# Pacing the second round of V loads with the heads in a cached-attention forward and backward kernel

## Chip, cores, metric

One core of a Trainium2 chip. The metric is device time in microseconds for one execution. All kernels here give the correct result.

## The reference

Gradients of one decode step of an adaLN block: attention with a KV cache, then a gated FFN. What fills the time is the cache:

```
x: (2, 1, 512)   k_cache, v_cache: (2 batches, 32 heads, 8192, 128) bf16, 128 MiB each
q = h @ wq;  p = softmax(q k^T / sqrt(128));  o = p v;  x = x + ga * (o @ wo);  x = x + gb * ffn(...)
returned: the output and the gradients of x, k_cache, v_cache, wq, wo, w1, w3, w2, c, w_mod
```

The gradient of each cache is as large as the cache: per head 2 MB of dV and 2 MB of dK are stored. V is needed twice, for o and again for the gradient of p, so all but two heads of V are loaded a second time.

## The kernel before

The program is laid out in slots, eight to a head. Heads of "job a" read K and V (forward). Heads of "job c" read V again and store dV and dK (backward). Between them stand two "chains", one per batch, that turn the attention output into the gradients that job c needs. After the second chain (slot t1 = 784) only job c is left: 32 heads in slots 768 to 1023, beside about 200 small tasks (weight gradients, which go out through staging tiles "stg").

All big data passes through 21 half tiles (1 MB each: half a head of K, V, dV or dK). Loads are issued by SP, in the order of need, as soon as the bookkeeping of the program has a free half tile (beyond a few that `keep` holds back for the stores):

```python
def load_v(key, i, hf):
    t = htile()
    qd.dma_start(t[:], src_of(A_v_cache, i)[:, hf * HK:(hf + 1) * HK, :])
    free["half"] -= 1
    V[(key, hf)] = t

def pump():
    while loads and free["half"] - keep[0] >= 1:
        loads.pop(0)[2]()          # (slot of need, sequence, load)
```

PE transposes V of the head (eight 128x128 blocks a slot), the half tile is then free. DVE makes dV and dK as outer products into other half tiles, and POOL stores them:

```python
def transposes(block, dve):
    tp = tps.tile([P, GRP, P], BF16, name="tp", tag="tp")
    for j in range(GRP):
        nc.tensor.transpose(tp[:, j, :], block(j), identb[:])
    kt = ktp.tile(...)                      # copied by ACT, or DVE in 2 slots of 8
def outer(store, dst, n, which, w2, q):
    ...                                     # cut
    nc.vector.tensor_tensor(...)            # 128x2048 outer product, two to a half tile
    if o + QK == HK:
        sq_.dma_start(src_of(dst, n)[...], t[:])       # sq_ is POOL
        at(now[0] + 6, PL_FREE, back)       # the half tile counts as free 6 slots later
def chain_done():                           # at slot t1
    ...                                     # the chain's weights give their half tiles back
    pump()
def again(w, n):                            # weights once more, for two last gradients
    for pc in range(n - 1, -1, -1):
        loads.insert(0, (0, 0, lambda pc=pc: load_piece(wqr, w, pc)))    # need 0: first in line
    pump()
```

By this bookkeeping the loads run 53 slots, over six heads, ahead of their use from slot 787 on: at t1 there is a burst of nine V loads, and afterwards about 13 of the 21 half tiles hold V that waits.

## Time and profile before

| | before |
|---|---|
| median of the first 6 runs | 1759.84 us (1757.52 to 1761.74) |
| profiled run | 1758.21 us, span 1756.4 us |
| bytes moved | 713.59 MB |

From the page of the kernel before: the busy share of the DMA engines in 40 slices of the span, what they moved, and the two big queues (q1 are the loads, q0 the stores).

```profile
DMA  9999999999999999999999999999999999999997
GB/s 381 418 417 416 418 417 390 418 377 414 382 411 422 413 414 410 420 410 409 410 413 409 409 420 403 382 371 419 424 413 419 409 405 417 413 421 423 420 402 293
q1 hardware_dynamic: 73376, 425.81, 60.0%
q0 software_dynamic: 41216, 284.22, 39.1%
```

The DMA is full from end to end: nothing else bounds this kernel.

From the kernel's waits, 1260 us to the end: who waited for whom, us in total, times, longest.

```profile
DVE half L1038 <- DMA out_dram<-half: 83.8, 40, 5.0
ACT stg L1163 <- DMA out_dram<-stg: 76.5, 20, 14.8
```

DVE waits 84 us for stores to land, because the loads hold most half tiles.

### The profile page before, as it was taken

What the parts mean: (1) busy time and instruction counts of PE and PEld (TensorE: products, weight loads), DVE (VectorE), ACT (ScalarE), POOL (GpSimd) and SP (SyncE); (2) the same over time, 40 slices, a digit from 0 to 9 for tenths busy, and PEclk for the clock granted to TensorE, in tenths of its full rate; (3) what the DMA queues carried; (4) which work ended last, traced back from release to release, by engine and by line L of the source; (5) the groups of instructions that cost most, each with busy time, mean ns of one, the idle gap of its engine ahead of it and who ended that gap; (6) DMA issues with size and microseconds to landing.
All of it is one profiled execution on the core that took longest, in us unless ns stands there. A gap on an engine that the chain in (4) does not pass through costs nothing. (4 is left out here: it accounts for less than half of the span.)

```text
span 1756.4 us, 55279 instructions
## 1 busy us (share of the span) xinstructions
PE 1371.6 (78%) x24266; PEld 1224.9 (70%) x24266; DVE 1181.3 (67%) x1697; ACT 953.2 (54%) x1370; POOL 391.6 (22%) x685
## 2 busy tenths in 40 slices
PE   5999999989887776668677767887678777866862
PEld 5999998888876666667576666787555555664662
DVE  2666665856767667667766767899566666665695
ACT  4666665653654454555455455434465566664762
POOL 0333333310222122222212222211012221111121
PEclk7999999989986888898888889668665555585785
DMA  9999999999999999999999999999999999999997
GB/s 381 418 417 416 418 417 390 418 377 414 382 411 422 413 414 410 420 410 409 410 413 409 409 420 403 382 371 419 424 413 419 409 405 417 413 421 423 420 402 293
DMA packets 114847, 713.59 MB, mean 406 GB/s; under 512 B 11392, under 2 KB 20300, under 8 KB 33196
## 3 DMA queue, kind: packets, MB, share of 16 engines
q1 hardware_dynamic: 73376, 425.81, 60.0%
q0 software_dynamic: 41216, 284.22, 39.1%
q8 instruction: 190, 3.11, 0.7%
q14 instruction: 53, 0.43, 0.1%
q10 hardware_dynamic: 12, 0.01, 0.0%
HBM read 425.79 MB, written 284.20 MB: 404 GB/s over the span
## 5 line engine op out<-in xcount | busy, mean ns | idle before, releaser
L371 ACT COPY kt<-tp 128x1024 bf16<-128x1024 bf16 x768 | 775.2, 1015 | 587.7 <-PE tp L366 574.3
L366 PE MATMUL tp<-identb,half 128*128 128x128 bf16 x8192 | 759.4, 248 | 4.2 <-DMA half<-in_A_k_cache_dram 1.9
L366 PEld LDWEIGHTS <-half 128*128 128x128 bf16 x8192 | 590.0, 111 | 113.6 <-issue 109.4
L1043 POOL DMA_DIRECT2D out_dram<-half x256 | 136.3, 532 | 983.0 <-DVE half L1038 798.9
L427 PE MATMUL m_ps<-ek,half 128*128 128x129 bf16 x4096 | 327.3, 222 | 0.2 <-DMA half<-in_A_v_cache_dram 0.2
L369 DVE COPY kt<-tp 128x1024 bf16<-128x1024 bf16 x256 | 176.2, 688 | 182.8 <-PE tp L366 181.1
L1015 PE MATMUL s_ps<-DO_bf,kt 128*128 128x1 bf16 x4096 | 190.1, 167 | 102.6 <-DVE kt L369 60.0
L1015 PEld LDWEIGHTS <-kt 128*128 128x128 bf16 x4096 | 184.4, 106 | 119.3 <-DVE kt L369 67.0
L386 PE MATMUL s_ps<-qT_bf,kt 128*128 128x1 bf16 x4096 | 177.8, 164 | 107.0 <-DVE kt L369 100.9
L427 PEld LDWEIGHTS <-half 128*128 128x128 bf16 x4096 | 247.8, 98 | 0.4 <-DMA half<-in_A_v_cache_dram 0.4
L386 PEld LDWEIGHTS <-kt 128*128 128x128 bf16 x4096 | 160.3, 98 | 113.0 <-DVE kt L369 105.0
L1163 ACT CAST stg<-m_ps 128x512 bf16<-128x512 f32 (+2 forms) x123 | 72.1, 592 | 107.7 <-DMA out_dram<-stg 76.5
L1162 PE MATMUL m_ps<-half 2*128 2x512 bf16 (+2 forms) x123 | 72.2, 587 | 23.5 <-ACT stg L1163 21.9
L449 PE MATMUL k_ps<-half,pz 128*32 128x512 bf16 x1024 | 67.4, 383 | 24.7 <-POOL pz L435 24.7
L449 PEld LDWEIGHTS <-pz 128*32 128x32 bf16 x1024 | 21.6, 96 | 45.3 <-POOL pz L435 27.0
L1263 ACT COPY kt<-tp 128x1024 bf16<-128x1024 bf16 x28 | 28.7, 1043 | 11.1 <-PE tp L1256 11.1
L398 DVE TENSOR_REDUCE nm<-s_ps 128x1 f32<-128x128 f32 x64 | 18.6, 290 | 20.1 <-PE s_ps L395 20.1
L1140 ACT CAST half<-m_ps 2x512 bf16<-2x512 f32 (+1 forms) x36 | 20.0, 564 | 22.4 <-DVE ds_26107 L1059 9.0
L1256 PE MATMUL tp<-identb,half 128*128 128x128 bf16 x224 | 21.6, 254 | 12.6 <-DMA half<-in_A_wq_dram 8.2
L395 PE MATMUL s_ps<-nident,rm 128*128 128x128 bf16 x64 | 14.8, 232 | 18.2 <-DVE rm L390 18.2
L1256 PEld LDWEIGHTS <-half 128*128 128x128 bf16 x224 | 16.7, 114 | 12.9 <-DMA half<-in_A_wq_dram 8.5
L714 DVE COPY kt<-tp 128x1024 bf16<-128x1024 bf16 x32 | 22.1, 690 | 4.2 <-PE tp L711 4.2
(870 smaller groups left out, 1792.3 us busy)
## 6 DMA issues: line engine op xcount, KB each, us to landing
out_dram<-half POOLq DMA_DIRECT2D x256, 1024.0 KB, 13.4
half<-in_A_v_cache_dram SPq DMA_DIRECT2D x252, 1024.0 KB, 12.5
half<-in_A_k_cache_dram SPq DMA_DIRECT2D x128, 1024.0 KB, 19.8
out_dram<-stg POOLq DMA_DIRECT2D x22, 512.0 KB, 16.8
half<-in_A_wq_dram SPq DMA_DIRECT2D x8, 1024.0 KB, 17.0
half<-in_w_mod_dram SPq DMA_DIRECT2D x6, 1024.0 KB, 16.6
half<-in_B_w_dram SPq DMA_DIRECT2D x6, 1024.0 KB, 15.4
half<-in_A_wo_dram SPq DMA_DIRECT2D x4, 1024.0 KB, 20.5
```

What stands on the lines that cost most here:

```text
L366: nc.tensor.transpose(tp[:, j, :], block(j), identb[:])
L369: nc.vector.tensor_copy(kt[:], tp[:])
L371: nc.scalar.copy(kt[:], tp[:])
L386: nc.tensor.matmul(S_ps[i][:, cc:cc + 1], kt[:, j, :], qT_bf[:, h, b:b + 1], start=True, stop=True)
L427: nc.tensor.matmul(m[:, 0:P + 1], vb_(i, kk), t[:, kk % QK, 0:P + 1], start=(kk == 0), stop=(kk == KK - 1), skip_group_check=True)
L449: nc.tensor.matmul(kp["ps"][NR * j:NR * (j + 1), :], pz[:, o:o + NR], K[(i, kk // HK)][:, kk % HK:kk % HK + QP, :], start=False, stop=(h = ...
L1015: nc.tensor.matmul(DP[n][:, cc:cc + 1], kt[:, j, :], DO_bf[:, b, h:h + 1], start=True, stop=True)
L1043: sq_.dma_start(src_of(dst, n)[:, hf * HK:(hf + 1) * HK, :], t[:])
L1162: nc.tensor.matmul(ps[:lw, 0:rw], rsl(ln, lc, lw), rsl(rn, rc, rw), start=True, stop=True)
L1163: nc.scalar.copy(st["t"][:lw, o:o + rw], ps[:lw, 0:rw])
L1256: nc.tensor.transpose(tp[:, k * NC + kc, :], piece(wqr, kc, m0 + k), identb[:])
L1263: nc.scalar.copy(kt[:], tp[:])
```

## The change

Its intent: after the second chain, load V only as it is needed, in lots of four half tiles, at most 12 slots (a head and a half) ahead, the first of each lot tied by a semaphore to the last PE transpose before it in the program. Half tiles are then left to the stores. The diff, whole but for the lines that only keep handles of the last load and the last transpose:

```diff
+    LOT = 4
+    AHEAD = NG + NG // 2              # NG is 8
+    paced = [False]
+
     def pump():
+        if paced[0] and loads and loads[0][0] > 0:
+            if loads[0][0] > now[0] + AHEAD:
+                return
+            if free["half"] - keep[0] < min(LOT, len(loads)) and loads[0][0] > now[0] + HG:
+                return
+            for k in range(min(LOT, len(loads), free["half"] - keep[0])):
+                issued[0] = None
+                loads.pop(0)[2]()
+                if k == 0 and issued[0] is not None:
+                    tc.add_manual_dep(issued[0].ins, turned_last[0].ins.name, ...,
+                                      reason="loads keep pace with the heads")
+            return
         while loads and free["half"] - keep[0] >= 1:
             loads.pop(0)[2]()
 ...
@@ def chain_done():
             rowst[k] = hflat()
             free["half"] -= 1
+        paced[0] = True
         pump()
```

In words: V loads due more than 12 slots ahead are held back, and so is a lot until four half tiles are free (unless its first load is due within HG, which is 4 slots).

At t1 V is in hand up to slot 804, so no load is due until slot 796: the burst of nine is gone. And a weight reload has need 0, so while one is first in line the old greedy path runs and takes V loads along: five V loads too early at slots 903 and at 954.

More of the change, by code (lines that the diff above doesn't have):

```diff
@@ L163 @@
     V = {}
+    issued = [None]
+    turned_last = [None]
     def src_of(ap, i):
@@ L176, in load_v @@
         t = htile()
-        qd.dma_start(t[:], src_of(A_v_cache, i)[:, hf * HK:(hf + 1) * HK, :])
+        issued[0] = qd.dma_start(t[:], src_of(A_v_cache, i)[:, hf * HK:(hf + 1) * HK, :])
         free["half"] -= 1
@@ L327, in want @@
         loads.append((need, seq[0], f))
+    LOT = 4
+    AHEAD = NG + NG // 2
+    paced = [False]
     def pump():
+        if paced[0] and loads and loads[0][0] > 0:
[7 more added lines that the diff above has]
+                if k == 0 and issued[0] is not None:
+                    tc.add_manual_dep(issued[0].ins, turned_last[0].ins.name,
+                                      mybir.DependencyInfo(mybir.DependencyClass.Sync, mybir.DependencyReason.DATA),
+                                      reason="loads keep pace with the heads")
+            return
         while loads and free["half"] - keep[0] >= 1:
@@ L365, in transposes @@
         for j in range(GRP):
-            nc.tensor.transpose(tp[:, j, :], block(j), identb[:])
+            turned_last[0] = nc.tensor.transpose(tp[:, j, :], block(j), identb[:])
         kt = ktp.tile([P, GRP, P], BF16, name="kt", tag="kt")
```

## The prediction

> **What bounds the kernel now.** The DMA. The utilisation slices show the DMA engines at 90% or more in 39 of 40 slices; the queue table gives 60.0% of the span to loads, 39.1% to stores. 713.59 MB must move whatever the order: at the best rate of any stretch (426 GB/s, 1260 to 1300 us, windows view) that is 1675 us; the span is 1756. PE is busy 78%, DVE 67%, ACT 54%.
>
> The change acts only after the second chain, in the last 490 us, where 32 heads each load 2 MB of V and store 4 MB. Windows view: 1260-1300: 426 GB/s, DMA 1.01; 1300-1650: 414 GB/s, 1.01, DVE busy 222 of 350; 1690-1750: 364 GB/s, 0.89, stores only, DVE busy 48 of 60. The last V load is issued at 1654.5 us, 100 us before the end: the slot bookkeeping lets loads run 53 slots (over six heads, 13 of the 21 half tiles) ahead. Stores have few half tiles left: in the waits view from 1260 us, DVE waits 84 us for earlier stores to land. This is not lost time: the DMA is full meanwhile.
>
> **What the change does.** No work or bytes change. It (a) holds V loads to 12 slots ahead, so some eight half tiles move from waiting V to stores in flight; (b) issues loads in lots of four, the first of each tied to a PE transpose; (c) leaves the greedy path while weight reloads wait, so the pacing breaks twice.
> - DVE's 84 us of waits should mostly go, into a longer store queue (landing 17 us now, perhaps 20 to 35). Worth about 0 with the DMA at 1.01.
> - A head costs about 16 us of DMA (6.3 MB plus weight gradients at 414 GB/s); DVE's own work is eight products of 1.22 us plus copies, about 12 us. So 12 slots ahead is 18 to 25 us (estimate), against 10.9 us median landing of a V load. PE should rarely wait for V.
> - Loads mixed into the end: stores alone ran at some 395 GB/s for 55 us (estimate from the last window without its empty end), mixed at 414 to 426: 2 to 4 us gained.
> - The burst of nine loads just after the chain goes; stores alone must fill the DMA for 12 slots, DVE-limited near 350 GB/s (4.2 MB per 12 us): 2 to 3 us lost.
> - Weight-gradient staging waits behind a deeper store queue (ACT already waits 76 us for it): 0 to 3 us lost.
>
> The Trainium skill, "DMA: Bandwidth & Descriptors", section "Queues, rings and completion order", says each engine takes turns between queues by packet; the trace roughly agrees (1260-1300: 7.47 MB loaded, 9.50 MB stored). So a lot of four is not stuck behind a deep store queue.
>
> **Prediction.** 1756 us, range 1744 to 1769. Faster by over 2%: 1%; within 2%: 95%; slower by over 2%: 4%.
>
> **What would show it.** Right: DMA share about 1.0 from 1300 us on, V loads issued until some 40 us before the end, DVE's wait for store landings well under 84 us, store landing over 17 us, end windows over 364 GB/s, PE waiting on V under 10 us. Wrong: windows with DMA share below 0.95, or PE transposes released by V loads.
>
> **What would make it wrong.** Slower: V loads land later than 12 slots because their buffers' stores have not landed, or the staging stores stall ACT and with it the transposes, so that the DMA runs dry between lots. Faster: lots of four and deeper store queues raise the mixed stretch from 414 towards 426 GB/s (up to 12 us), which I do not expect, since 50/50 and 25/75 mixes look nearly alike.

## More of the kernel before

From the kernel before, the last 560 us; in each row the stretch and its length, busy time (and instructions) of PE, PEld, DVE, ACT and POOL, then the granted PE clock, the DMA share and GB/s.

```profile
core 0: us, PE busy (x) PEld busy (x) DVE busy (x) ACT busy (x) POOL busy (x), PEclk, DMA share, GB/s
1200.00:1240.00 40.00, 32.22 (x544) 30.64 (x544) 36.34 (x78) 17.69 (x25) 5.31 (x10) 0.71 1.01 424
1240.00:1270.00 30.00, 17.94 (x264) 15.24 (x262) 14.86 (x18) 12.96 (x21) 3.19 (x6) 0.67 1.01 425
1270.00:1450.00 180.00, 137.42 (x1477) 101.20 (x1477) 114.00 (x121) 107.62 (x179) 35.55 (x62) 0.54 1.01 411
1450.00:1650.00 200.00, 147.52 (x1821) 114.38 (x1819) 124.81 (x139) 124.04 (x187) 33.42 (x63) 0.61 1.02 418
1650.00:1690.00 40.00, 30.65 (x600) 28.71 (x599) 30.75 (x34) 30.64 (x41) 6.37 (x12) 0.84 1.00 414
1690.00:1770.00 80.00, 26.65 (x480) 25.10 (x478) 48.02 (x50) 23.08 (x31) 10.10 (x19) 0.70 0.67 273
```

(The span ends at 1756.4, so the last row is 66 us of work and an empty rest.) The rate hardly leaves 411 to 425 GB/s before the stores-only end.

## The result, and the profile after

| | before | after |
|---|---|---|
| median | 1759.18 us (20 runs, 1756.47 to 1763.58) | 1766.54 us (10 runs, 1758.79 to 1768.92) |
| ratio | | 1.0034, 95% interval 1.0022 to 1.0046 |
| profiled run | 1758.21 us | 1760.47 us |

Ratios, here and below, are the mean time of one kernel's fast runs over the mean of the other's from the same rounds, so not quite the ratio of the medians.

The kernel is a third of a per cent slower: inside the predicted range, on the other side of zero than its centre. Its runs lie in two clusters, three at 1758.8 to 1761.5 us and seven at 1765 to 1769 us; the profiled run is of the shorter one.

The page of the kernel after, the same two lines of slices:

```profile
DMA  9999999999999999999999999999999999999997
GB/s 382 417 417 417 418 417 389 418 377 408 382 408 423 419 422 417 406 413 411 416 414 414 407 409 410 384 370 418 365 419 412 417 412 420 423 423 422 369 424 322
```

The digits are the same, the rates are not: slice 29 fell from 424 to 365 GB/s and slice 38 from 420 to 369. The windows of the kernel after (same columns):

```profile
1200.00:1240.00 40.00, 32.52 (x548) 30.97 (x546) 35.45 (x77) 16.29 (x21) 5.53 (x11) 0.69 0.98 409
1240.00:1270.00 30.00, 26.80 (x426) 22.59 (x425) 29.49 (x32) 28.09 (x47) 5.84 (x11) 0.84 0.92 358
1270.00:1450.00 180.00, 142.60 (x1526) 105.29 (x1524) 116.66 (x126) 112.11 (x185) 36.70 (x64) 0.54 1.01 416
1450.00:1650.00 200.00, 129.40 (x1722) 103.87 (x1719) 110.03 (x125) 110.40 (x162) 29.77 (x56) 0.60 1.01 420
1650.00:1690.00 40.00, 29.63 (x579) 27.78 (x578) 35.31 (x39) 29.91 (x42) 7.96 (x15) 0.83 0.94 372
1690.00:1770.00 80.00, 20.04 (x352) 18.50 (x348) 38.19 (x40) 16.96 (x22) 7.97 (x15) 0.66 0.73 308
```

There are two holes, and in each the load stream had paused. In the first, SP issued no load from 1208 to 1252 us (the trace of DMA issues); its waits over 1205 to 1275 us name the tie, and windows of 10 us show how deep the hole was:

```profile
SPq L179 <- PE tp L385: 46.0, 2, 43.5
1230.00:1240.00 10.00, 8.49 (x170) 8.23 (x168) 8.06 (x17) 4.21 (x7) 1.59 (x3) 0.67 0.89 365
1240.00:1250.00 10.00, 9.63 (x165) 8.23 (x163) 9.90 (x11) 9.21 (x16) 1.59 (x3) 0.88 0.77 312
1250.00:1260.00 10.00, 8.39 (x134) 7.24 (x132) 9.97 (x12) 9.45 (x16) 2.12 (x4) 0.83 0.98 339
```

By the packets, no load moved a byte from 1223 to 1255 us. DVE was busy nearly throughout from 1240 us on (9.90 and 9.97 of 10 us): from there the stores went as fast as DVE could make them.

In the second hole SP issued none from 1602 to 1661 us. Between the holes and at the end the kernel after is the faster one.

A ledger makes this countable. For each window, take its length times (1 - rate / 424), with 424 GB/s as the full rate: the DMA time that the window gave away. The last window is cut at the end of the span.

| DMA us given away | 1200-1240 | 1240-1270 | 1270-1450 | 1450-1650 | 1650-1690 | 1690-end | sum |
|---|---|---|---|---|---|---|---|
| before (1758.2 us) | 0 | 0 | 5.5 | 2.8 | 0.9 | 14.9 | 24.1 |
| after, shorter cluster (1760.5 us) | 1.4 | 4.7 | 3.4 | 1.9 | 4.9 | 10.5 | 26.8 |
| after, longer cluster (1765.4 us, the look below) | 5.3 | 6.6 | 3.8 | 0.9 | 5.8 | 10.0 | 32.4 |
| pacing 16 slots later (1758.8 us, below) | 0 | 0 | 7.6 | 1.4 | 4.1 | 12.0 | 25.1 |

The sums differ from before by 2.7, 8.3 and 1.0 us, the spans by 2.2, 7.2 and 0.7. So the table holds nearly the whole difference. (As all kernels move the same bytes, it must, if they are alike up to 1200 us: it says where the time went, not why.)

What was expected of the waits did come. From 1260 us to the end, the kernel after:

```profile
POOL out_dram L1062 <- DMA out_dram<-half: 124.1, 40, 4.7
ACT stg L1182 <- DMA out_dram<-stg: 113.0, 24, 18.5
DVE half L1057 <- DMA out_dram<-half: 8.2, 3, 3.9
```

DVE's 84 us of waiting went down to 8. It did not become time: POOL, which issues the stores, now waits 124 us for earlier stores to land, and ACT waits 113 us in place of 77 for its staging tiles.

### The profile page after: what moved, and what is told of

Same layout as the page of the kernel before. It is cut to its first block, busy times and chain, and to the rows that moved or that the text cites. A ratio compares the mean times of both kernels' runs of the same rounds, so it can differ in the third digit from the quotient of the medians.

```text
span 1758.6 us, 55264 instructions
## 1 busy us (share of the span) xinstructions
PE 1374.3 (78%) x24266; PEld 1235.9 (70%) x24266; DVE 1179.3 (67%) x1697; ACT 952.5 (54%) x1370; POOL 391.6 (22%) x685
## 5 line engine op out<-in xcount | busy, mean ns | idle before, releaser
L385 PE MATMUL tp<-identb,half 128*128 128x128 bf16 x8192 | 769.8, 250 | 4.6 <-DMA half<-in_A_v_cache_dram 1.8
L405 PEld LDWEIGHTS <-kt 128*128 128x128 bf16 x4096 | 160.0, 98 | 111.1 <-DVE kt L388 104.4
L1034 PEld LDWEIGHTS <-kt 128*128 128x128 bf16 x4096 | 190.5, 108 | 63.5 <-issue 26.9
L468 PE MATMUL k_ps<-half,pz 128*32 128x512 bf16 x1024 | 67.4, 384 | 24.1 <-POOL pz L454 24.1
L414 PE MATMUL s_ps<-nident,rm 128*128 128x128 bf16 x64 | 15.4, 241 | 19.1 <-DVE rm L409 19.1
L1275 PE MATMUL tp<-identb,half 128*128 128x128 bf16 x224 | 19.7, 240 | 11.1 <-ACT kt L390 11.1
L730 PE MATMUL tp<-identb,half 128*128 128x128 bf16 x256 | 26.3, 266 | 0.0
```

The costliest lines, as they stand in the source:

```text
L385: turned_last[0] = nc.tensor.transpose(tp[:, j, :], block(j), identb[:])
L405: nc.tensor.matmul(S_ps[i][:, cc:cc + 1], kt[:, j, :], qT_bf[:, h, b:b + 1], start=True, stop=True)
L468: nc.tensor.matmul(kp["ps"][NR * j:NR * (j + 1), :], pz[:, o:o + NR], K[(i, kk // HK)][:, kk % HK:kk % HK + QP, :], start=False, stop=(h = ...
L1034: nc.tensor.matmul(DP[n][:, cc:cc + 1], kt[:, j, :], DO_bf[:, b, h:h + 1], start=True, stop=True)
L1275: nc.tensor.transpose(tp[:, k * NC + kc, :], piece(wqr, kc, m0 + k), identb[:])
```

## The experiments

Theory: V loads taken far ahead are the reserve that keeps the DMA full while the heads are slow. With pacing, loads and stores both follow the heads, so each stretch of slow heads leaves the DMA short. Rivals: lots of four are the harm (bursts delay the staging stores); the tie to a transpose is the harm; or a pause costs nothing in itself, and the loss belongs to the handover after the chain.

(The 10 us rates quoted in the expectations are on the clock of the packet records, which is about 10 us ahead of the span's.) The first four kernels ran together; before had a median of 1760.0 us beside them (11 runs).

**24 slots ahead in place of 12.**

```diff
-    AHEAD = NG + NG // 2
+    AHEAD = 3 * NG
```

> The kernel after with loads up to 24 slots ahead in place of 12 (nothing else). My theory, holes in the load stream: just after the chain the profiled kernel after issues no load from 1208 to 1252 us while 12 slots pass, and the stores alone ran at 310 to 361 GB/s (1240 to 1260 us), some 6 us of DMA time lost; with 24 slots the first lot comes at once and this hole goes, so every 10 us stretch from 1230 to 1300 us should move over 400 GB/s, the hole near 1660 us shrinks, and the ratio to before should be about 0.999 to 1.001, against 1.0034. Rival, lots of four are the harm (bursts delay the staging stores, ACT waits 113 us for them in place of 76): the lots are the same, so the ratio stays near 1.003. Rival, the tie of a lot to a transpose is the harm: unchanged too, near 1.003.

Measured: 1759.35 us, ratio 0.9998 (0.9984 to 1.0011). The loss is gone, but not as I said. Its windows:

```profile
1200.00:1240.00 40.00, 35.88 (x487) 34.80 (x485) 33.86 (x72) 15.77 (x23) 4.78 (x9) 0.50 0.91 370
1240.00:1270.00 30.00, 26.89 (x485) 23.65 (x484) 28.30 (x36) 24.77 (x39) 5.31 (x10) 0.82 0.98 385
1650.00:1690.00 40.00, 30.59 (x605) 28.56 (x603) 35.27 (x39) 30.91 (x41) 7.16 (x14) 0.84 1.00 411
```

The second hole is gone. The first is shorter (no load byte for 20 us in place of 32) but stays, because it begins before slot 784: the loads of V up to slot 804 had all been issued by 1214 us, and PE reached slot 784 at 1242 us. A lot that is planned at 784 cannot come earlier. The burst of before did: the trace has its loads issued from 1218 us on, as half tiles came free. This profile shows PE at half clock in the first window and was the longest of its six runs (1763.3 us), so how deep its first hole is tells little about the distance.

**Weight reloads that do not break the pacing.**

```diff
+        while paced[0] and loads and loads[0][0] == 0 and free["half"] - keep[0] >= 1:
+            loads.pop(0)[2]()
+        if paced[0] and loads and loads[0][0] == 0:
+            return
         if paced[0] and loads and loads[0][0] > 0:
```

> The kernel after, but the weight reloads no longer break the pacing: only they are issued at once, V loads keep to 12 slots. Theory of the holes: the second hole (342 and 306 GB/s at 1660 to 1680 us, no load issued from 1602 to 1661 us, some 5 us of DMA time lost) goes, since it is the wait for the heads to catch up with nine loads taken in one go; the first hole at 1240 to 1260 us stays. Ratio to before about 1.000 to 1.002. Rivals (lots or tie): no change, near 1.003.

Measured: 1764.4 us, ratio 1.0022 (1.0010 to 1.0034); 1240 to 1270 us at 320 GB/s, 1650 to 1690 at 386. A miss: the second hole got no smaller than in other runs of the kernel after (372, 387 and 363 GB/s in its three profiles), so the lump of loads taken too early was not its main cause. The heads there are slow, among the last weight tasks: by the starts of their first transposes, the heads of slots 944, 952 and 968 take 23 to 26 us each in the kernel after. In before the head of slot 952 takes 27 us and that of 968 20, and loads far ahead covered it. But the change makes them slower still: the four heads of slots 944 to 968 take 90.5 us together in the kernel after, 76.3 in before. In these stretches (1563 to 1654 us, and 1586 to 1662 in before) ACT waited 41 us in place of 25 for the small stores of the weight gradients to land, and PE 36 us in place of 16 for ACT. That is the chain that the prediction names under "What would make it wrong": staging stores stall ACT and with it the transposes, so that the DMA runs dry between lots. The traces fit it; no run isolates it.

**Both edits.**

> Both edits: 24 slots ahead, and weight reloads that do not break the pacing. Theory of the holes: neither hole is left, DMA share about 1.0 in every window from 1230 us to the end, and what the change gains by mixing loads into the last stretch (421 to 425 GB/s in place of about 400 over the last 55 us, some 3 us) is left over: ratio 0.996 to 0.998. Rivals (lots or tie): still near 1.003.

Measured: 1763.09 us, ratio 1.0012 (0.9996 to 1.0027). Both holes are still there (382 GB/s over 1240 to 1270 us, 359 over 1650 to 1690). A miss. The first hole stays for the reason given above. That the second stays is not explained: 24 slots ahead alone had closed it (411). The last loads before it were issued at 1640 to 1642 us there and at 1626 to 1629 us here, so where the lots happen to fall may matter. The rival "lots" does not fit either: with 24 slots ahead, same lots and same ties, the loss was gone.

**No tie.**

```diff
-                if k == 0 and issued[0] is not None:
+                if False:
```

> The kernel after without the tie to a transpose: the same order and the same lots of loads in the program, but at run time a load waits only for its buffer. Theory of the holes: with 12 of 21 half tiles free in the bookkeeping, loads run ahead at run time as far as buffers allow, so the first hole goes and the run looks like before with more room for stores: ratio 0.998 to 1.000. Rival, lots of four or the smaller store share are the harm: near 1.003. If the tie does nothing (buffers set the pace anyway), the ratio is 1.003 and the holes stay.

Measured: 1759.93 us, ratio 0.9995 (0.9982 to 1.0008). The second hole is gone (422 GB/s) and the first begins to close earlier (367 GB/s, then 406), since SP issues the first lot at 1238 us in place of 1252. So the tie has a share in both holes: it is what makes a planned pause a real one. The rival "tie" is thus half right: neither the short distance nor the tie does the harm without the other.

The next four ran together, before at 1758.34 us (11 runs).

**The kernel after once more.**

> The kernel after once more, unchanged, for its spread (1758.8 to 1768.9 us in two clusters) and for a profile of the other cluster. Theory: the longer runs are those where PE had the half clock in slots 760 to 784 (about 1180 to 1240 us): the heads of those slots then take 17.2 us each in place of 14 to 16, the stores and the ties come later, and with no load in hand the DMA idles longer; the kernel before has loads in hand there and does not care. If the profile falls in the long cluster it should show PE clock 0.5 in 1200 to 1240 us and a deeper first hole (under 320 GB/s over 1240 to 1260 us); if in the short one, clock 0.6 or more. Median 1764 to 1767 us, ratio 1.002 to 1.005.

Measured: 1763.46 us (just under what I expected), ratio 1.0025 (1.0007 to 1.0043), in the same two clusters, three runs at 1758.9 to 1760.5 and three at 1766.4 to 1768.0 us. The profile fell in the shorter one: clock 0.73 over 1200 to 1240 us, 421 GB/s there and 359 in the hole.

**Pacing starts 16 slots later, so the burst stays.**

```diff
-        paced[0] = True
         pump()
+    def pace():
+        paced[0] = True
     at(t1, PL_TASK, chain_done)
+    at(t1 + 16, PL_TASK, pace)
```

> The kernel after, but the pacing starts 16 slots later, so that the burst of loads just after the chain is made as before and the pause of the loads comes afterwards and is longer (44 slots without a load being issued, in place of 13). Theory of the holes: no hole at 1230 to 1270 us; the store-only stretch moves to somewhere in 1300 to 1380 us, with DMA below 400 GB/s there; the loads are only put off, so the ratio stays above 1.001 (up to 1.005). Rival, the harm is particular to the handover after the chain (PE and ACT busy with weight gradients, half clock): ratio back to 1.000 or below.

Measured: 1757.99 us, ratio 0.9992 (0.9979 to 1.0005), and one cluster (1756.5 to 1758.8). Its windows over the first hole, the pause and the second hole:

```profile
1240.00:1270.00 30.00, 17.46 (x248) 14.87 (x245) 14.86 (x18) 13.87 (x23) 2.73 (x6) 0.67 1.01 425
1300.00:1360.00 60.00, 57.69 (x586) 42.37 (x586) 48.04 (x49) 42.47 (x69) 16.53 (x28) 0.50 1.01 393
1650.00:1690.00 40.00, 29.54 (x556) 27.27 (x552) 36.20 (x40) 28.78 (x38) 7.43 (x14) 0.83 0.96 381
```

Here the theory as I first had it failed, and the rival won: the pause became longer (44 slots) and yet cost little, 393 GB/s against 412 in the kernel after in those 60 us. A pause is cheap where heads are quick (13.8 us each, with weight gradients besides). It is dear at the handover, where the heads up to slot 784 took 14 to 17 us each with no weight gradient yet to store: 4.2 MB in 14 to 17 us is 250 to 300 GB/s (worked out), and between 1230 and 1260 us the windows of 10 us have 312 to 365 GB/s in the kernel after and 256 to 327 in its longer run below. Putting back the burst took away all of the loss, although the second hole stayed.

**Lots of one.** `LOT = 1` in place of 4, nothing else.

> The kernel after with lots of one load in place of four, each tied to a transpose, still 12 slots ahead. Theory of the holes: the loads pause just as long, both holes stay, ratio 1.002 to 1.005. Rival, lots of four are the harm (small dips to 380 GB/s before each lot; staging stores late): ratio 1.000 or below, and no dips in 1300 to 1450 us.

Measured: 1767.66 us, ratio 1.0048 (1.0035 to 1.0061), at the top of the range I gave. The first hole is there as expected (336 GB/s over 1240 to 1270 us), so it does not need lots of four. The second is not where I expected it (423 over 1650 to 1690 us); instead 1450 to 1650 us ran at 410 GB/s, for a reason of its own. Its waits over 1495 to 1560 us:

```profile
PE tp L385 <- DMA half<-in_A_v_cache_dram: 24.8, 1, 24.8
```

With one load at a time, V for slot 916 and after stood behind the four weight reloads of slot 903, and PE starved for 25 us. So pacing close to the need leaves no room for a queue-jumper. Because of that loss the time of this run does not measure lots alone.

**A version meant to beat both: a shrinking distance.** After the burst, single tied loads, at most `max(12, 53 - 41 * (now - t1) // 220)` slots ahead; weight reloads do not break it.

> A version meant to beat both: the burst after the chain as before without ties, then the distance that loads may run ahead shrinks evenly from 53 slots to 12 by the end, one load at a time, and weight reloads do not break it. Theory of the holes: loads never pause, so no hole at 1230 to 1270 us and none near 1660 us; the last loads are issued some 50 us before the end, so the last stretch is mixed or has a deep store queue (over 415 GB/s in 1690 to 1745 us in place of 395); ratio 0.995 to 0.998. If the mixing at the end is worth nothing, 1.000; if pacing itself harms, 1.002 or more.

Measured: 1756.83 us, ratio 0.9993 (0.9981 to 1.0005). No hole (424 GB/s over 1240 to 1270, 418 over 1650 to 1690), and no gain that can be told from nothing: 1270 to 1450 us ran at 411 GB/s and 1450 to 1650 at 418, exactly as before.

The last four ran together, before at 1758.6 us (11 runs).

**The pause alone, in the kernel before.** In before, no loads for slots 784 to 795; the first load at 796 tied to the last transpose; then greedy again, no pacing, no lots.

```diff
     def pump():
+        if pause[0]:
+            return
+        if pause[1] and ...:      # once, at t1 + 12: one load, tied to the last transpose
         while loads and free["half"] - keep[0] >= 1:
@@ chain_done
-        pump()
+        pause[0] = True           # lifted at t1 + 12
```

> The kernel before with one thing of the change alone: no loads for 12 slots after the second chain, the first load after the pause tied to a transpose of slot 796; then greedy as before, no pacing. Theory, now put as: loads taken far ahead are what fills the DMA while the heads are slow (16 to 17 us a head up to slot 784, whose stores alone are 4.2 MB in that time, 250 to 260 GB/s): the first hole alone costs what it idles, 5 us with PE at 0.6 to 0.8 clock there and 10 to 12 us at 0.5, and nothing wins it back: ratio 1.002 to 1.006, DMA under 360 GB/s over 1240 to 1265 us, and all later windows as in before. If a load put off can be made up later for nothing (DMA work is conserved, as I predicted), 1.000.

Measured: 1761.9 us, ratio 1.0025 (1.0004 to 1.0046), the same ratio as the whole change gave in its second measurement, and the same two clusters: 1757.7 to 1759.2 and 1764.6 to 1767.8 us. Its profile fell in the shorter one:

```profile
1200.00:1240.00 40.00, 32.41 (x556) 30.44 (x555) 36.62 (x78) 17.89 (x24) 5.85 (x11) 0.72 0.97 402
1240.00:1270.00 30.00, 23.66 (x403) 19.62 (x400) 23.92 (x25) 27.84 (x47) 4.25 (x8) 0.90 0.94 371
```

So the first pause by itself is enough for a loss of this size and for the two clusters. (Before has a weak trace of the longer one: two of its eleven runs beside this one took 1763.6 and 1764.8 us.) In the shorter cluster the pause costs about nothing: the burst that follows ran at 418 GB/s over 1270 to 1450 us against 411 in before, which by the ledger wins back 3.0 of the 5.8 us that the first two windows gave away. My expectation had said that nothing would; for that cluster it was wrong.

**Both slow stretches filled.** Pacing from t1 + 16, reloads apart, and 32 slots ahead from slot 896 on.

> The kernel after with both slow stretches given loads to fill them: pacing starts 16 slots after the chain (burst as before), loads may run 32 slots ahead from slot 896 on in place of 12, and weight reloads do not break the pacing; lots of four and ties as in after. Theory: no hole at 1240 to 1270 us and none at 1650 to 1680 us (both windows over 415 GB/s), and what the change wins elsewhere (stores at over 420 GB/s at the end in place of 395, 420 or more in 1450 to 1650 in place of 417) is left over: ratio 0.996 to 0.998. If the second hole has another cause than loads being held back, it stays and the ratio is 0.999.

Measured: 1758.15 us, ratio 0.9995 (0.9981 to 1.0009). The first hole is gone (424 GB/s), the second is down to one stretch of 10 us (401 over 1650 to 1690 us). The gain I expected is not there: the store-only pause after the burst gives away 7.6 us in 1270 to 1450 us where before gives away 5.5, and the end gives away 14.5, about as in before (14.9).

**The shrinking distance in lots of four.**

> The shrinking distance of the earlier run (53 to 12 slots) but in lots of four, pacing from 16 slots after the chain. If lots of four themselves raise the rate of the mixed stretch (421 to 423 GB/s in 1450 to 1650 us with lots, 410 to 418 with single loads), ratio 0.996 to 0.998 and 1450 to 1650 us over 420; if the rate has to do with the depth of the store queue and not with lots, like the single loads, 0.999.

Measured: 1758.78 us, ratio 0.9997 (0.9984 to 1.0010), 418 GB/s over 1450 to 1650 us. Lots do not raise the rate by themselves; 420 to 422 was seen there in the kernels with lots that hold loads to 12, 24 or 32 slots. A second hole is there too (381 GB/s over 1650 to 1690 us), again with no loss in the time.

**A look at the longer cluster.** The kernel after, one profiled run and no rounds.

> The kernel after once more, for a profile of its longer cluster (1764 to 1769 us; it falls there about six times in ten). If it does: PE clock 0.5 in 1180 to 1240 us, 17 us a head in slots 760 to 784, first hole under 320 GB/s in 1240 to 1270 us and 10 us of DMA time lost there, second hole as in the shorter one. If the long cluster showed the fast clock there, my account of the two clusters falls.

It fell in the longer cluster: 1765.43 us (a single run, state unknown). Its windows:

```profile
1200.00:1240.00 40.00, 34.54 (x486) 33.33 (x483) 34.56 (x75) 16.76 (x24) 5.20 (x10) 0.54 0.90 368
1230.00:1240.00 10.00, 8.14 (x112) 7.84 (x112) 8.56 (x21) 4.46 (x7) 1.48 (x3) 0.50 0.63 256
1240.00:1250.00 10.00, 9.74 (x180) 9.04 (x180) 8.63 (x14) 5.79 (x8) 1.18 (x3) 0.61 0.71 292
1240.00:1270.00 30.00, 28.02 (x497) 24.81 (x498) 28.46 (x35) 25.14 (x40) 5.43 (x11) 0.81 0.85 331
1650.00:1690.00 40.00, 30.62 (x610) 28.61 (x609) 35.01 (x39) 30.87 (x41) 7.42 (x14) 0.84 0.92 363
```

PE had 0.54 of its clock over 1200 to 1240 us, in place of 0.69 and 0.73 in the two profiles of the shorter cluster. The trace has the heads of slots 760 to 776 at 16.4 to 17.0 us each, against 14.1 to 16.3 in the other profile of this kernel that ran beside before. So the hole is deeper, if not quite under the 320 GB/s that I expected: 11.9 us given away in the first two windows, against 6.1. That is most of the distance between the clusters. The clock differs before the pause begins: over 1180 to 1200 us it was 0.58 here and 0.89 in the first profile of this kernel, and the last load before the pause was issued at 1213 and 1208 us. So the low clock is not an effect of the pause.

## Why the prediction was right and wrong

- **The DMA is the bound, and bytes do not change.** Right; it is why all kernels here lie within half a per cent.
- **DVE's 84 us of waits are worth about nothing.** Right. They fell to 8 us, and POOL (124 us) and ACT (113 us) wait in its place.
- **PE should rarely wait for V; V loads land in time.** Right for the change itself (1.8 us). It is no general safety: lots of one starved PE for 25 us.
- **"Loads mixed into the end: 2 to 4 us gained."** Right, a little small: the end gives away 10.5 us in place of 14.9, and the two long middle windows 3 us less.
- **"Stores alone must fill the DMA for 12 slots, DVE-limited near 350 GB/s: 2 to 3 us lost."** This is the step that failed. The pause was named but mis-sized: the two windows gave away 6.1 us in the shorter cluster and 11.9 in the longer. In the shorter cluster the rate was about as said (361 GB/s over 1224 to 1254 us, DVE busy 27.4 of the 30); the length was not. Twelve slots at 12 us a head are 18 us, but no load was issued for 44 us: SP had issued all loads planned before slot 784 by 1208 us, PE reached that slot at 1235 us, and the tie then held the next lot until 1252. In the longer cluster the stores were alone for longer and the rate fell too (307 GB/s over 1224 to 1260 us), behind heads at 16.4 to 17.0 us. Seven of ten runs were of the longer cluster, so the median carries the larger number. The pause alone put into before gives 1.0025; taken out of the change, 0.9992.
- **"The pacing breaks twice", and DMA share about 1.0 from 1300 us on.** Not costed, and false: the windows of 1650 to 1690 us have 0.94 and 372 GB/s, 4.9 us given away against 0.9. That hole went with 24 slots ahead (411 GB/s), and without the tie (422); it stayed with 24 slots and the reloads out of the way (359), and with these out of the way alone (386). The heads in front of it are slow in before too, and slower here.
- **"Weight-gradient staging waits: 0 to 3 us lost."** The waits came (ACT 113 us in place of 77). What they cost by themselves is not measured: they are part of what slows the heads in front of the second hole.
- **The signs.** Store landings went from 17 to 23 us, as predicted. "V loads issued until some 40 us before the end" failed: the last was issued at 1683 us, 76 us before the end (102 us in before).
- **The sum.** By the ledger, a gain of 7 to 8.5 us in the middle and the end, less 4 to 5 us for the second hole, less 6 to 12 for the first, is a loss of 3 to 8 us in place of the small gain predicted. The time lay within the range of 1744 to 1769 us because the range was wide, not because the terms were right.

Open: why PE is granted half its clock in slots 760 to 784 in some runs and not in others. The link of clock and cluster rests on profiles (0.54 in the longer run of the kernel after, 0.69 and 0.73 in the shorter ones, and 0.50 and 0.54 in the profiles of three variants that keep the first pause and took 1765 us or more; against it, the kernels without the tie and with 24 slots ahead had 0.50 and took 1759.6 and 1763.3, with no second hole); before was not profiled at half clock, so what that clock costs without a pause is not known, and the longer cluster of the pause-alone kernel was not profiled at all. Six variants have ratios of 0.9992 to 0.9998 with intervals of about 0.0013 to each side; none is shown to beat before, nor any one another.

## What to carry to other kernels

Where the DMA is the bound, as in this kernel, work that is fetched far ahead is not waste of buffers but a reserve: it fills the DMA while compute is slow, and a load stream that is paced by compute goes slack just when the store stream does. Before cutting a look-ahead, find the stretches where compute is slowest, work out what the stores alone move there, and keep enough loads in hand to cover them. A wait of an engine behind a full DMA, even one of 84 us, is no prize.

## What the Trainium skill lacked or had wrong

- "TensorE: Matmul & The Clock Gate", Part 1, says that activity releases the throttle, and that the warm-up at a kernel's start varies from run to run but costs under 1% of a typical kernel. Here, in the middle of the kernel, the same program had a mean clock of 0.73 in one run and 0.54 in another over 1200 to 1240 us, with PE busy 32.3 and 34.5 of the 40 us (a slower clock by itself makes PE busy for longer). Part 4 of that page says that transposes do not count as busy in the same way; whether that plays a part, no run here isolates. The page does not say that a stretch of some 60 us in mid-kernel (0.78 and 0.55 over 1180 to 1240 us) can go either way between runs of one program; the two clusters that go with it here lie about 7 us of 1760 apart.
- "HBM Reference", "Specifications (TRN2)", gives about 425 GB/s for a core that streams alone. The windows agree (424 to 426 GB/s at the best), for loads and stores together. No page says how the mix matters: 409 to 418 GB/s with a third of it loads and small staging stores among them, and stores alone at 403 GB/s in 1690 to 1740 us of before but 424 in 1712 to 1740 us of the kernel after, where more stores were in flight (landing 19.1 us after issue in place of 13.1).
- "DMA: Bandwidth & Descriptors", "Queues, rings and completion order": turns between queues by packet. The trace agrees: over 1240 to 1270 us of before the load queue moved 6.32 MB and the store queue 6.39. What it costs a load to stand behind others of its own queue has no number there: V loads behind four weight reloads landed after 31 us in place of 11 (lots of one).
